# Linear attention and two dense layers on one core: tail projections in row tiles, and a new order of the attention period

## The chip, the cores and the metric

The kernel runs on one core of a Trainium2 chip. The metric is the device time of one execution in microseconds (us), as the median over several runs. TensorE multiplies matrices, VectorE reduces and combines, ScalarE copies and applies functions, GpSimd does elementwise work, and SyncE (SP) issues nearly all transfers. "Array" is TensorE's 128x128 array; a product of 64 rows uses half of its rows, an output of 64 or 32 partitions a part of its columns.

## The reference

```python
def phi(x):
    proj = np.einsum('bhsd,df->bhsf', x, w_phi)
    proj = proj - np.max(np.abs(proj), axis=-1, keepdims=True)
    return np.concatenate([np.exp(proj), np.exp(-proj)], axis=-1)
q_p, k_p = (phi(q), phi(k))
kv = np.einsum('bhsf,bhsd->bhfd', k_p, v)
z = np.sum(k_p, axis=2)
num = np.einsum('bhsf,bhfd->bhsd', q_p, kv)
den = np.einsum('bhsf,bhf->bhs', q_p, z)[..., None] + 1e-06
...
h = x @ w_in
g = h * (1.0 / (1.0 + np.exp(-h)))
return (g @ w_out).astype(np.float32)
```

There are 4 batches of 8 heads, 576 positions, 64 numbers per head and 128 features. The attention output becomes 2304 rows of 512; two dense layers of width 2048 follow, the second with h * cos(h). All is fp32.

## The kernel before

The attention is worked in eight groups `n` of four heads each. Of the 576 positions 512 are the main part and 64 the tail. For one group and one of q and k, `phi` (line 366) projects: `u == 0` is the tail of all four heads, `u == 1` and `u == 2` the main part of two heads each. A main call issues eight products (L380) of 64 rows by 128 columns, in pairs: one takes partitions 0 to 63, the other 64 to 127, and they write the two halves of a PSUM tile `p` of two banks (tag "p", two buffers, so four banks). The tail is one product (L372) over all 128 partitions with 256 columns, against `wf`, a weight of which two quarters are zero (the two heads of a partition block stand in it block by block); it writes one bank of the tag "t2" (two buffers). VectorE then takes the maximum of the absolute values (L384) and subtracts it (L386); the PSUM buffer is free when the subtraction is done.

The other pieces of one group are:

- `kx.u` (k_exp, L402): ScalarE's two exponentials of a k part.
- `qx.u` (q_exp): TensorE transposes of a q part into a "t2" tile (L410, four for the main part, two for the tail), and ScalarE's exponentials (L417, L420).
- `kv.p.c.h` (kv_parts): products for the key-value matrix of head pair `p`, feature half `c`, first or second part `h`. The first part begins with two products of the tail (L436) and goes on with eight of the main part (L439), the second has eight more. They have 64 output columns of the array, and after the last ScalarE copies the result (L443).
- `num.a.half` (L458, four products, 64 columns) and `den.half` (L469, eight products, 32 columns), each into a buffer of the tag "kn" (two buffers, shared with kv) and copied out by ScalarE (L279, L285).
- `load.k`, `load.q`, `load.v`: transfers issued on SP. A group's v goes into `va` (L338, one buffer) and `vt` (L341, two buffers), so most of v can be loaded only when the kv products of the group before are done.
- `inv`, `app`: the reciprocal of `den`, sent through memory to all partitions, and the multiplication with it (GpSimd, L308 and L311), after whose second call for a batch `xd` is stored (L313).
- `piece`: one step of preparing the dense layers' weights (a fetch of raw weights, L139 and L141; an operation or two on ScalarE, VectorE or GpSimd; a store, L199).
- `x.i`: one step of the first dense layer's inputs, in the last two periods.

The order in which the pieces are issued, the same for all engines, is written out by hand in two tables. START is run once and holds the first group's beginning. PERIOD is run for n = -1 to 7; `+` after a name means the next group, `++` the one after. Steps that START already did are skipped. Every engine works its own instructions in that order, and semaphores order them between engines. After the eighth period `moe` begins with products L757.

Of the kernel before, what the change touches and what calls it, by code (L numbers as in the profile page):

```python
# [7 lines left out]
F32 = mybir.dt.float32  # L8
# [7 lines left out]
P = 128  # L16
NQ = 8
B, H, S, D = 4, 8, 576, 64
F = 128
# [14 lines left out]
PB, T2, KN, QB = 2, 2, 2, 2  # L34
# [13 lines left out]
def parse(text):  # L48

    out = []  # L50
    for w in text.split():
        name, *args = w.rstrip("+-").split(".")
        out.append((w.count("+") - w.count("-"), name, *(int(x) if x.isdigit() else x for x in args)))
    return out
# [8 lines left out]
""")  # L63

PERIOD = parse("""
kv.1.1.1 phi.k.2+ num.0.1 num.0.0 num.1.1 load.v+ kx.1+ x.3+ phi.q.1+ den.0 piece x.5+ den.1 num.1.0 phi.q.0+ qx.1+
piece inv kx.2+ kx.3+ phi.q.2+ x.4+ phi.k.1++ kv.0.0.0+ kx.4+ kv.0.0.1+ qx.0+ kv.0.1.0+ piece x.0+ kv.0.1.1+ x.2+
load.q++ qx.2+ x.7++ app.G qx.3+ kv.1.0.0+ x.1++ load.k+++ kv.1.0.1+ x.6+ qx.4+ phi.k.0++ x.8++ kx.0++ kv.1.1.0+ piece
""")


# [244 lines left out]
def attention(tc, q, k, v, w_phi, norm, pieces, then):  # L316
    nc = tc.nc
    W = D + 1
    with ExitStack() as ctx:
# [3 lines left out]
        pp = ctx.enter_context(tc.tile_pool(name="at_ps", bufs=1, space=PSUM))  # L323
# [19 lines left out]
        wf = sp.tile([P, 2 * F], F32, name="wf")  # L343
# [23 lines left out]
        def phi(n, name, u):  # L367

            src = raw[n, name]
            if u == 0:  # L370
                pt = pp.tile([P, 4, P], F32, name="t2", tag="t2", bufs=T2)[:, 0:2]
                nc.tensor.matmul(pt.rearrange("p a f -> p (a f)"), src[:, 0:P], wf, start=True, stop=True)  # L372
                pv, g = pt, 2
            else:
                ps = pp.tile([P, 2, 4, F], F32, name="p", tag="p", bufs=PB)
                c = P + (u - 1) * SM
                for i in range(4):
                    for half in range(2):
                        rows = slice(D * half, D * half + D)
                        nc.tensor.matmul(ps[:, half, i], src[rows, c + i * P:c + (i + 1) * P], wf[rows, half * F:(half + 1) * F],  # L380
                                         start=True, stop=True)
                pv, g = ps.rearrange("p a b f -> p (a b) f"), 8
            m = sp.tile([P, g], F32, name=f"m{g}", bufs=3)
            nc.vector.tensor_reduce(m, pv, axis=AX.X, op=ALU.max, apply_absolute_value=True)  # L384
            t = sp.tile([P, g, F], F32, name="pmt" if u == 0 else "pm", bufs=2 if u == 0 else 3)
            nc.vector.tensor_tensor(t, pv, m.unsqueeze(2).to_broadcast([P, g, F]), op=ALU.subtract)  # L386
            pm[n, name, u] = t
# [87 lines left out]
        def step(n, name, *arg):  # L475
# [14 lines left out]
            elif name == "phi":  # L490
                phi(n, *arg)
            elif name == "kx":
                k_exp(n, *arg)
            elif name == "qx":
                q_exp(n, *arg)
            elif name == "kv":
                p, c, h = arg
                if (n, p) not in kvq:
                    kvq[n, p] = kv_parts(n, p)
                for f in kvq[n, p][9 * c + 5 * h:9 * c + 5 + 4 * h]:  # L500
                    f()
            elif name == "num":
                num(n, *arg)
            elif name == "den":
                den(n, *arg)
            elif name == "warm":
                t = pp.tile([P, 512], F32, name="num", tag="kn", bufs=KN)
                for _ in range(arg[0]):
                    nc.tensor.transpose(t[:, 0:P], ident, ident)
            elif name == "inv":  # L510
                norm.invert(n)
            elif name == "app":
                norm.apply(n, engines[arg[0]])
# [636 lines left out]
```

## Time and profile before

| | us |
|---|---|
| median of 3 runs (941.54 to 944.22) | 941.57 |
| the profiled execution, its own time | 941.5 |
| its span, first to last instruction | 939.4 |
| TensorE busy | 929.7 |
| VectorE busy | 639.5 |
| ScalarE busy | 522.3 |
| GpSimd busy | 173.2 |

The attention lasts to about 165.6 us of the span, the dense layers take the rest. Positions in the text are us from the start of the span. "The chain" is the chain of waits that ended last, followed back through the program: a piece of it on TensorE lasts from the end of the piece before it to its own end, so its lengths add up. The granted TensorE clock of the whole run is 1.00.

### The profile page before, as it was taken

The numbers are of one execution on the slowest core, as the hardware profiler recorded it, in microseconds if no ns is written. First come the engines' busy times: TensorE is split into PE (matmuls) and PEld (weight loads), VectorE is DVE, ScalarE is ACT, GpSimd is POOL, SyncE is SP. The second block draws the span as 40 slices with busy tenths as digits, with TensorE's granted clock in tenths as the row PEclk, the third lists the DMA queues.
The fourth block names the chain that finished last, engine by engine and source line by source line (L and its number), as shares of the span: only waits on it lengthen the run. The fifth ranks groups of instructions, "written<-read, shape, count | busy, mean of one in ns | idle before, by whom it ended". The sixth has DMA issues, their size and how long they took to land.

```text
span 939.4 us, 18064 instructions
## 1 busy us (share of the span) xinstructions
PE 929.7 (99%) x7271; PEld 813.9 (87%) x7271; DVE 639.5 (68%) x961; ACT 522.3 (56%) x944; POOL 173.2 (18%) x142
## 2 busy tenths in 40 slices
PE   8999999999999999999999999999999999999998
PEld 7777776889899998999888988988988989889996
DVE  5777656886647568874456688588786796556556
ACT  4666767866444455565544557463644556544452
POOL 0112342017261711532512500000000000000000
PEclk9999999999999999999999999999999999999999
DMA  5654665566555569798878774633466356342402
GB/s 169 214 141 104 171 193 169 163 231 243 176 225 180 218 227 321 270 370 305 306 277 317 258 291 180 209 128 135 170 226 232 117 198 224 112 157 90 136 1 89
DMA packets 95490, 186.52 MB, mean 199 GB/s; under 512 B 27952, under 2 KB 56752, under 8 KB 94640
## 3 DMA queue, kind: packets, MB, share of 16 engines
q1 hardware_dynamic: 95264, 185.25, 57.6%
q8 instruction: 57, 0.93, 0.4%
q14 instruction: 25, 0.20, 0.1%
q10 hardware_dynamic: 144, 0.13, 0.0%
HBM read 128.06 MB, written 57.22 MB: 197 GB/s over the span
## 4 chain that ended last, share of the span: by engine, by line
PE 97%; DMA 1%; DVE 1%; ACT 1%; issue 0%; SPq 0%
PE h L757 38%; PE y L826 7%; PE y L828 7%; PE y L827 7%; PE y L833 7%; PE y L832 7%; PE y L831 7%; PE p L380 4%; PE num L458 3%; PE kv L439 3%; PE t L410 2%; PE num L469 2%; PE kv L436 1%; PE t L372 1%; DMA vt<-in_v 0%; DMA wf<-in_w_phi 0%
## 5 line engine op out<-in xcount | busy, mean ns | idle before, releaser
L757 PEld LDWEIGHTS h<-xo,w 128*128 128x128 f32 x2688 | 330.0, 188 | 11.6 <-DVE u L970 2.2
L757 PE MATMUL h<-xo,w 128*128 128x256 f32 x2688 | 334.5, 281 | 2.0 <-DVE u L970 1.1
L826 PE MATMUL y<-gh,w 128*128 128x512 f32 (+1 forms) x320 | 119.3, 373 | 0.0
L828 PE MATMUL y<-gh,w 128*128 128x512 f32 (+1 forms) x320 | 118.9, 372 | 0.0
L827 PE MATMUL y<-gl,w 128*128 128x512 f32 (+1 forms) x320 | 118.7, 371 | 0.0
L833 PE MATMUL y<-w,gl 128*128 128x512 f32 x288 | 113.9, 395 | 0.0
L832 PE MATMUL y<-w,gh 128*128 128x512 f32 x288 | 113.6, 394 | 0.0
L831 PE MATMUL y<-w,gh 128*128 128x512 f32 x288 | 113.4, 394 | 0.0
L777 DVE TENSOR_TENSOR gl<-ta,gh 128x512 fp32r<-128x512 f32 x72 | 62.2, 863 | 61.1 <-ACT gh L775 61.0
L782 ACT ACTIVATE tb<-tb 128x512 f32<-128x512 f32 x72 | 45.6, 634 | 92.6 <-DVE tb L781 92.6
L861 DVE TENSOR_TENSOR xa<-y,xa 128x512 f32<-128x512 f32 (+1 forms) x114 | 70.5, 655 | 23.7 <-PE y L828 17.5
L781 DVE SCALAR_TENSOR_TENSOR tb<-tb,ta 128x512 f32<-128x512 f32 x72 | 49.3, 685 | 48.9 <-ACT tb L791 48.9
L191 POOL TENSOR_TENSOR w<-stage,w 128x512 fp32r<-128x512 f32 x48 | 66.7, 1400 | 42.3 <-ACT w L187 36.3
L828 PEld LDWEIGHTS y<-gh,w 128*128 128x128 f32 x320 | 60.1, 188 | 11.2
L826 PEld LDWEIGHTS y<-gh,w 128*128 128x128 f32 x320 | 60.2, 188 | 9.5 <-ACT xa L859 0.2
L827 PEld LDWEIGHTS y<-gl,w 128*128 128x128 f32 x320 | 60.2, 188 | 9.4
L833 PEld LDWEIGHTS y<-w,gl 128*128 128x128 f32 x288 | 54.0, 188 | 12.8
L832 PEld LDWEIGHTS y<-w,gh 128*128 128x128 f32 x288 | 54.0, 188 | 10.8
L831 PEld LDWEIGHTS y<-w,gh 128*128 128x128 f32 x288 | 54.1, 188 | 10.5
L191 POOL TENSOR_TENSOR w<-wt,w 128x512 fp32r<-128x512 f32 x24 | 39.7, 1656 | 125.6 <-ACT w L187 125.6
L775 ACT CAST gh<-ta 128x512 fp32r<-128x512 f32 x72 | 44.7, 621 | 27.8 <-PE y L828 26.0
L235 POOL TENSOR_TENSOR stage<-stage 128x512 f32<-128x512 f32 x28 | 40.7, 1454 | 82.2 <-DVE stage L179 81.8
(103 smaller groups left out, 1384.9 us busy)
## 6 DMA issues: line engine op xcount, KB each, us to landing
w<-d SPq DMA_DIRECT2D x48, 512.0 KB, 5.4
raw_in<-in_moe_w_in SPq DMA_DIRECT2D x32, 512.0 KB, 5.8
raw_out<-in_moe_w_out SPq DMA_DIRECT2D x32, 512.0 KB, 4.5
d<-w SPq DMA_DIRECT2D x32, 512.0 KB, 5.9
rb<-rd SPq DMA_DIRECT2D x16, 288.0 KB, 4.5
va<-in_v SPq DMA_DIRECT2D x32, 128.0 KB, 6.0
yd<-xa SPq DMA_DIRECT2D x4, 1024.0 KB, 3.9
xo<-yd SPq DMA_DIRECT2D x32, 128.0 KB, 4.8
```

The source lines that it names most:

```text
L191: e.tensor_sub(lo, t, hi.bitcast(F32))
L757: nc.tensor.matmul(dst[:, ab], w[:, a, ab, c * P:(c + 1) * P], o[:, b, idx, c], start=start and n == 1, stop=n == 12, skip_group_check=True)
L777: return [silu, lambda: nc.vector.tensor_sub(lo, a, hi.bitcast(F32))]
L781: nc.vector.scalar_tensor_tensor(b, b, MAGIC, a, op0=ALU.subtract, op1=ALU.subtract)
L782: nc.scalar.activation(b, b, AF.Sin, scale=-2.0 * math.pi)
L826: nc.tensor.matmul(o, w[:, 0, at], hi[:, f, x], stop=False, **st)
L827: nc.tensor.matmul(o, w[:, 0, at], lo[:, f, x], start=False, stop=False)
L828: nc.tensor.matmul(o, w[:, 1, at], hi[:, f, x], start=False, stop=en)
L831: nc.tensor.matmul(o, hi[:, f, at], w[:, 0], stop=False, **st)
L832: nc.tensor.matmul(o, hi[:, f, at], w[:, 1], start=False, stop=False)
L833: nc.tensor.matmul(o, lo[:, f, at], w[:, 0], start=False, stop=en)
L861: nc.vector.tensor_tensor(v, o, v, op=ALU.add)
```

## The change

The tail projection becomes two products of 64 rows by 128 columns, one for each half of the partitions, without the zero quarters of `wf`. They write the first block of each half of a "p" tile, so the tail no longer uses "t2". The table PERIOD is written in another order; START is the same.

```diff
 PERIOD = parse("""
-kv.1.1.1 phi.k.2+ num.0.1 num.0.0 num.1.1 load.v+ kx.1+ x.3+ phi.q.1+ den.0 piece x.5+ den.1 num.1.0 phi.q.0+ qx.1+
...
+phi.k.2+ kv.1.1.1 piece num.0.1 num.1.1 phi.q.0+ x.3+ load.v+ kx.1+ phi.q.1+ den.0 den.1 kx.4+ num.0.0 x.5+ num.1.0
...
             if u == 0:
-                pt = pp.tile([P, 4, P], F32, name="t2", tag="t2", bufs=T2)[:, 0:2]
-                nc.tensor.matmul(pt.rearrange("p a f -> p (a f)"), src[:, 0:P], wf, start=True, stop=True)
+                pt = pp.tile([P, 2, 4, F], F32, name="p", tag="p", bufs=PB)[:, :, 0]
+                for a in range(2):
+                    rows = slice(D * a, D * a + D)
+                    nc.tensor.matmul(pt[:, a], src[rows, 0:P], wf[rows, a * F:(a + 1) * F], start=True, stop=True)
                 pv, g = pt, 2
```

TensorE, around the border of two periods, before: the transposes of `qx.4`, the tail and then the main part of k (`phi.k.0`, `phi.k.2`) with the last kv product group between them, the three `num`, and `phi.q.1` (kr and qr are the loaded k and q, kv the key-value products, t the transposes).

```order
L410 MATMUL t_973<-ident,pm 128x128 x4
L372 MATMUL t_980<-wf,kr 128x256
L436 MATMUL kv<-vt_206,kpt 64x130 x2
L439 MATMUL kv<-va,kp 64x65 x16
L380 MATMUL p<-wf,kr 128x128 x8
L458 MATMUL num<-qh_836,kv_931 64x288 x8
L458 MATMUL num<-qh_837,kv_1010 64x288 x4
L380 MATMUL p<-wf,qr 128x128 x8
```

The same place in the changed kernel (its lines are two higher from L374 on):

```order
L412 MATMUL t_992<-ident,pm 128x128 x4
L374 MATMUL p<-wf,kr 128x128 x2
L382 MATMUL p<-wf,kr 128x128 x8
L441 MATMUL kv<-va,kp 64x65 x8
L460 MATMUL num<-qh_846,kv_939 64x288 x4
L460 MATMUL num<-qh_847,kv_1030 64x288 x4
L374 MATMUL p<-wf,qr 128x128 x2
L382 MATMUL p<-wf,qr 128x128 x8
```

Tail and main part of k now stand side by side, as do tail and main part of q; the last kv part runs straight into two of the `num`, and the third `num` has moved behind `den`.

TensorE, in the middle of a period, before: `phi.q.2` and `phi.k.1`, then kv of the first head pair in two parts with the tail's transposes between them, and four transposes twice.

```order
L380 MATMUL p<-wf,qr 128x128 x8
L380 MATMUL p<-wf,kr 128x128 x8
L436 MATMUL kv<-vt_206,kpt 64x130 x2
L439 MATMUL kv<-va,kp 64x65 x16
L410 MATMUL t_903<-ident,pmt 128x128 x2
L436 MATMUL kv<-vt_206,kpt 64x130 x2
L439 MATMUL kv<-va,kp 64x65 x16
L410 MATMUL t_935<-ident,pm 128x128 x4
L410 MATMUL t_945<-ident,pm 128x128 x4
```

And in the changed kernel:

```order
L412 MATMUL t_864<-ident,pmt 128x128 x2
L382 MATMUL p<-wf,qr 128x128 x8
L382 MATMUL p<-wf,kr 128x128 x8
L438 MATMUL kv<-vt_206,kpt 64x130 x2
L441 MATMUL kv<-va,kp 64x65 x16
L438 MATMUL kv<-vt_206,kpt 64x130 x2
L441 MATMUL kv<-va,kp 64x65 x16
L412 MATMUL t_944<-ident,pm 128x128 x4
L412 MATMUL t_951<-ident,pm 128x128 x4
```

The tail's transposes have moved ahead, next to those of `qx.1`, and the two kv parts stand together.

SyncE's queue in the sixth period, where the next group's v is loaded behind the store of `xb`, before and then after:

```order
L331 DMA qr<-in_q 128x1152
L313 DMA xd_66<-xb 128x2048
L199 DMA d00S_77<-w_165 128x1024
L338 DMA va<-in_v 128x4x64 x4
L341 DMA vt_207<-in_v 64x64 x4
```

```order
L331 DMA qr<-in_q 128x1152
L199 DMA d00S_77<-w_165 128x1024
L313 DMA xd_66<-xb 128x2048
L338 DMA va<-in_v 128x4x64 x4
L341 DMA vt_207<-in_v 64x64 x4
```

The store of a prepared weight has moved ahead of the store of `xb`.

## Rows read from the trace of the kernel before

**Rows 1.** The page's first part: busy time of each engine.
```profile
PE 929.7 (99%) x7271; PEld 813.9 (87%) x7271; DVE 639.5 (68%) x961; ACT 522.3 (56%) x944; POOL 173.2 (18%) x142
```
**Rows 2.** The chain over one period: start us, us, what.
```profile
43.89 1.09 PE p L380 x16
44.98 3.06 PE num L458 x24
...
49.13 2.08 PE num L469 x32
51.21 1.12 PE num L458 x8
52.33 0.63 PE t L372 x2
...
53.40 1.98 PE p L380 x32
55.38 0.37 PE kv L436 x4
55.75 0.94 PE kv L439 x32
56.69 0.37 PE t L410 x2
...
58.37 1.02 PE t L410 x8
...
60.69 0.59 PE t L410 x4
61.28 0.53 PE t L372 x2
...
63.11 1.09 PE p L380 x16
```
**Rows 3.** The chain at the end of START.
```profile
22.91 0.47 PE kv L439 x16
23.38 0.59 PE t L410 x4
23.96 0.62 PE kv L439 x16
```
**Rows 4.** TensorE's instructions in order of time, in START.
```profile
18.45 0.39 PE L436 MATMUL kv<-vt,kpt 128*64 128x130 f32 x4
18.67 0.64 PE L439 MATMUL kv<-va,kp 128*64 128x65 f32 x16
```
**Rows 5.** VectorE's instructions in order of time, after k's tail and main projection.
```profile
42.62 0.42 DVE L384 TENSOR_REDUCE m<-t 128x2 f32<-128x256 f32 x1 [1.28 <-PE t L372]
...
45.03 1.23 DVE L384 TENSOR_REDUCE m<-p 128x8 f32<-128x1024 f32 x1 [0.93 <-PE p L380]
46.29 1.23 DVE L386 TENSOR_TENSOR pm<-p,m 128x1024 f32<-128x1024 f32 x1
```
**Rows 6.** ScalarE's instructions in order of time, in the same place.
```profile
43.62 0.72 ACT L402 ACTIVATE kpt<-pmt 128x256 f32<-128x256 f32 x2 [0.35 <-DVE pmt L386]
44.25 0.36 ACT L443 COPY kv<-kv 128x260 f32<-128x260 f32 x1
```
**Rows 7.** The chain at the last period's projection, and at the dense layers' start.
```profile
140.02 1.09 PE p L380 x16
...
165.60 3.03 PE h L757 x24
```
**Rows 8.** TensorE's instructions in order of time, before the last group's kv.
```profile
152.18 0.44 PE L436 MATMUL kv<-vt,kpt 128*64 128x130 f32 x4 [1.56 <-DMA vt<-in_v]
```
**Rows 9.** TensorE's waits up to 165 us: for what, us in total, times, longest.
```profile
PE kv L436 <- DMA vt<-in_v: 1.6, 1, 1.6
```
**Rows 10.** SyncE's issues in order of time, in the sixth period.
```profile
142.17 0.32 SPq L313 DMA_DIRECT2D xd<-xb  x1
```
**Rows 11.** The chain at the start of the span.
```profile
4.43 1.22 PE t L372 x2
```

More of the change, by code (lines that the diff above doesn't have):

```diff
@@ L65 @@
 PERIOD = parse("""
-kv.1.1.1 phi.k.2+ num.0.1 num.0.0 num.1.1 load.v+ kx.1+ x.3+ phi.q.1+ den.0 piece x.5+ den.1 num.1.0 phi.q.0+ qx.1+
-piece inv kx.2+ kx.3+ phi.q.2+ x.4+ phi.k.1++ kv.0.0.0+ kx.4+ kv.0.0.1+ qx.0+ kv.0.1.0+ piece x.0+ kv.0.1.1+ x.2+
-load.q++ qx.2+ x.7++ app.G qx.3+ kv.1.0.0+ x.1++ load.k+++ kv.1.0.1+ x.6+ qx.4+ phi.k.0++ x.8++ kx.0++ kv.1.1.0+ piece
+phi.k.2+ kv.1.1.1 piece num.0.1 num.1.1 phi.q.0+ x.3+ load.v+ kx.1+ phi.q.1+ den.0 den.1 kx.4+ num.0.0 x.5+ num.1.0
+piece qx.1+ inv kx.2+ kx.3+ x.4+ qx.0+ phi.q.2+ phi.k.1++ kv.0.0.0+ kv.0.0.1+ kv.0.1.0+ piece load.q++ x.0+ kv.0.1.1+
+piece qx.2+ qx.3+ x.2+ x.7++ app.G kv.1.0.0+ kv.1.0.1+ x.1++ load.k+++ x.6+ kv.1.1.0+ qx.4+ phi.k.0++ x.8++ kx.0++
 """)
```

## The prediction

> **What bounds the kernel now.** I read the page's busy times first: TensorE is busy 929.7 of 939.4 us and no other engine over 68% [rows 1], so what counts is how TensorE's time is filled. Then I read the chain of waits through the attention, the only stage that the change touches. Through a whole period it never leaves TensorE: from 43.89 to 63.11 us one piece follows another, 19.22 us in all [rows 2]. Up to 165 us TensorE waits for loaded v once, 1.56 us before the last group's kv [rows 8, 9], and its other waits there lie in START. A saving therefore has to come out of the lengths of those pieces, and a new wait costs in full.
>
> The pieces hold something that is no work. One main projection takes 1.09 us, two in a row 1.98 [rows 2]: the second costs 0.89, so 0.20 of the first is something else. Three `num` take 3.06 and one 1.12: 0.97 each, and 0.15 once. Eight transposes take 1.02 and two 0.37: 0.108 each, and 0.15 once. A half kv part after transposes takes 0.62, after its own kind 0.47 [rows 3]: 0.15 again. The two tail products of kv take 0.37 after another kind [rows 2], but 0.22 after kv (18.45 to 18.67) [rows 4]: 0.15. So a change of tile size (64 rows, 64 columns, 32 columns, whole array) costs 0.15 us, and 0.20 into 64 rows, while pieces of one size join at no cost. By the order, a period has 14 such changes before and 11 after.
>
> **The tails.** L372 takes 0.63 us behind `num`: 0.20 for its change and 0.43 of work. Behind transposes, where no change is due, it takes 0.53 [rows 2], 0.10 more than its work; I read that as a wait for its "t2" buffer. The pair of 64-row products isn't in the trace. Eight main products of its shape are four pairs in 0.89 us, so a pair takes 0.22 if it runs together, and 0.43 if it doesn't. I take 0.22, as the main products are the same instruction, and keep 0.43 for the range.
>
> **One period, summed.** In the new order, each size change in front of its piece: tail of k 0.42, main 0.89, second half of the last kv part 0.62, two `num` 1.94, tail of q 0.42, main 0.89, two `den` 2.08, two `num` 2.09, six transposes 0.80, two main projections 1.98, kv 1.30 and 1.15, eight transposes 1.02, kv 1.30, half a part 0.69, four transposes 0.59. That is 18.18 us, 1.04 less than 19.22: 0.42 from two tails, 0.1 from the "t2" wait, 0.5 from three size changes.
>
> **All periods.** Before, from the last kv half of START (23.96) to the dense layers (165.60) [rows 3, 7] are 141.64 us, of which 1.56 is the wait for v, so 140.08 of work. After: the first period lacks the tail of k, which START has done (17.96); five whole ones (90.90); the seventh lacks the main projection of a next group (17.29); the eighth has only the last kv half, `num` and `den` (0.62 + 1.94 + 2.08 + 2.09 = 6.73). Sum 132.88: **7.2 us less**.
>
> **The wait for v.** The last v is late since SP holds its loads behind the store of `xb`, issued at 142.17 [rows 10], and v lands just before 152.18, some 10 us later [rows 8]. That store hangs on the chain den, reciprocal, broadcast and GpSimd, none of it shortened. From `den` to the kv that needs v TensorE now takes about 22.2 us, where it had 22.5, so the wait would grow to 1.9. But a weight store of 512 KB now stands ahead of `xb`'s, not between it and v, and can be gone before. I take 0.8, with 0 and 1.9 as ends: **0.8 us less**.
>
> **START.** Its first tail takes 1.22 us [rows 11], a pair 0.22; what follows waits partly for VectorE and ScalarE. The gain lies between 0 and 1.4 (the 1.0, and 0.4 of a wait between transposes for "t2", which the tail leaves). I take **0.5 less**.
>
> **New waits.** The tails move into the two buffers of "p", six calls a period where four were. The main q projection now needs the buffer of the main k projection two calls before. VectorE starts to read that at its end (44.98 to 45.03) and is done 2.54 us later, at 47.52 [rows 5]. In the new order 0.62 + 1.94 + 0.42 = 2.98 us lie between, and a product starts up to 0.25 earlier than my ends show, so 0.2 is left. The second `num` now follows the kv group after one `num`. Its copy stands on ScalarE behind the exponentials of the k tail (43.62) and ends at 44.61 [rows 6], 2.0 us after VectorE has begun on that tail at 42.62 [rows 5]; 0.89 + 0.62 + 0.97 = 2.48 lie between, so again some 0.2. Both hold on paper with nothing to spare. I charge 0.1 per period, **0.7 us more**.
>
> Here the Trainium skill speaks against the change: "TensorEngine Tiling (Array Packing)", Gotcha 1: PSUM Pressure, says that row tiling raises the demand on PSUM, since different row tiles write different banks. The trace agrees so far that a two-bank tile is held 2.5 us after its projection. By that rule the sum would be the one of the second rival.
>
> **What else is moved.** In the first period four weight fetches of 512 KB go onto SP ahead of v instead of behind it; SP reaches them while TensorE is still in START, so they can run early. Later a weight fetch or store stands before a load of k; k is needed a period later. GpSimd gets one addition of weights ahead of `app` in some periods, at cost nothing since it is busy 18% [rows 1]; if that cover fails, `xb` and the last v come 1.3 us later. The dense layers' instructions keep their order, so they only shift.
>
> **Sum.** 7.2 + 0.8 + 0.5 - 0.7 = 7.8 us less than the profiled execution's own 941.5, which stands 0.07 under the median: 933.7 us.
>
> **The rivals.**
> - *The new order saves nothing.* If the 0.15 and 0.20 belong to each kind of piece and not to the size, only the tails save: 14 in the periods by 0.21, and START's 0.5, 3.4 in all: 938.1. For it: the price into 64 rows is not that of the others. Against it: the half kv part and the kv tail products show both lengths for the same piece.
> - *"p" becomes the bound.* The tail of k now ends just ahead of the main part, and VectorE reads it first, in two operations of 0.42 us [rows 5]. If the main part's read-out comes later by those 0.8 us in each period, less the 0.2 spare, the q projection waits 0.6 us instead of 0.1; seven times 0.5 is 3.5: 937.2. For it: the read-out of the tail does stand in front. Against it: the main products run 0.89 us, in which VectorE can finish the tail.
> - *v comes late in every period: slower.* The new order leaves 10.2 us between the end of kv and the next group's kv; most of v can be loaded only in there. In the last period the landing came 12.1 us after that end (140.02 to about 152.1) [rows 7, 8]. At that lag each of seven loads costs 1.9 us, 13.4 in all: 947.1. It decides against the change from a mean lag of about 11.4 us on, where seven times 1.2 us eat the gain. Against it: of all loads before only one was waited for [rows 9], and that one stood behind `xb`.
> - *The change doesn't do what it says:* the pair runs one after the other. That costs 0.21 for each of 14 tails, 2.9 us: 936.6.
>
> **How the numbers follow.** The forecast gets 0.64, the order that saves nothing 0.10, "p" as the bound 0.12, late v 0.06, the serial pair 0.04; 0.04 is left for losses at the start of the dense layers. The low end is the forecast with no wait for v (0.8), START at its best (0.9) and no new waits (0.7): 931.3. The high end takes in the first two rivals and the serial pair: 938.5. Faster by over 0.3% (which is about what a measurement can tell from no change) means under 938.7: 0.86, nearly all of the cases but late v. Within 0.3%: 0.08. Slower: 0.06, late v.
>
> **What would show it.** In the chain a period should be near 18.2 us, the main projections behind a tail 0.89 instead of 1.09, kv behind kv 1.15 instead of 1.30, two transposes of the tail no longer a piece of their own. TensorE should have no wait for VectorE at the q projection, and the one for v should be shorter. The dense layers should start near 157.8 us. A period near 18.7 with VectorE as releaser means the second rival, one of 19 us with whole pieces at their old lengths the first, and waits for v in many periods the third. I would be wrong altogether if the periods shortened and the dense layers took the time back.

## The result and the profile after

The changed kernel takes 932.58 us (median of 4 runs, 931.74 to 932.8), the kernel before beside it 941.56 (4 runs, 940.28 to 944.22): a ratio of 0.9899, 95% interval [0.9877, 0.9922], 9.0 us less. Two more measurements of the same kernel gave 932.61 and 931.92 (ratios 0.9897 [0.9879, 0.9915] and 0.9889 [0.9872, 0.9905]). The forecast was 933.7, with a range of 931.3 to 938.5.

The profiled execution's own time is 931.74, its span 929.6. The busy times on the page, against [rows 1]:

```profile
PE 919.8 (99%) x7303; PEld 809.2 (87%) x7303; DVE 641.5 (69%) x961; ACT 521.8 (56%) x944; POOL 170.1 (18%) x142
```

TensorE has lost 9.9 us of busy time, the span 9.8. Its idle time is the same in sum (9.7 and 9.8 us): new waits stand where the one for v was, and the saving lies in TensorE's pieces, which became shorter. Not all of that is the edit: TensorE ran the beginning of START at a higher rate in this execution (see below). The chain of waits over one period (start us, us, what) answers to [rows 2]; a product of the program counts twice in these rows, so x16 is the eight products of a main part, while a transpose counts once:

```profile
40.60 0.89 PE p L382 x16
41.49 0.61 PE kv L441 x16
42.11 1.94 PE num L460 x16
44.05 0.42 PE p L374 x4
44.47 0.89 PE p L382 x16
45.37 2.08 PE num L471 x32
47.44 2.09 PE num L460 x16
49.53 0.81 PE t L412 x6
...
53.63 0.22 PE kv L438 x4
53.85 0.93 PE kv L441 x32
...
58.39 0.42 PE p L374 x4
58.81 0.89 PE p L382 x16
```

The period runs from 40.60 to 58.81, 18.21 us, where it took 19.22. Both main projections behind a tail take 0.89 instead of 1.09, kv behind kv 0.22 + 0.93 = 1.15, six transposes in one piece 0.81, and the two products of a tail 0.42, of which 0.20 is their size change. No engine but TensorE stands in this stretch. The chain at the end of the last period and the start of the dense layers, against 165.60 in [rows 7]:

```profile
150.30 0.29 ACT kv L445
...
150.63 1.19 PE num L460 x8
...
155.99 3.04 PE h L759 x24
```

The dense layers start 9.61 us earlier. From there to the end are 773.6 us, where there were 773.8, with the same busy times of every engine to within 3 us: they only shifted. Part of the 9.61 lies in START: its last four transposes end at 22.19 instead of 23.96 [rows 3], 1.77 less. From there to the dense layers are 133.80 us instead of 141.64, 7.84 less. TensorE's waits up to 170 us (for what, us in total, times, longest), against [rows 9], which was the wait for v:

```profile
PE p L374 <- DVE pm L388: 0.9, 1, 0.9
...
PE p L382 <- DMA qr<-in_q: 0.7, 1, 0.7
...
PE num L460 <- ACT kv L445: 0.4, 1, 0.4
```

The first two lie in START. The third is new: in the last period the second `num` waits for the copy at 150.30. The wait for v is gone: against [rows 8], no wait stands behind the first kv row of the last group.

```profile
142.43 0.44 PE L438 MATMUL kv<-vt,kpt 128*64 128x130 f32 x4
```

### The profile page after: what moved, and what is told of

Same layout as the page of the kernel before. It is cut to its first block, busy times and chain, and to the rows that moved or that the text cites. A ratio compares the mean times of both kernels' runs of the same rounds, so it can differ in the third digit from the quotient of the medians.

```text
span 929.6 us, 18114 instructions
## 1 busy us (share of the span) xinstructions
PE 919.8 (99%) x7303; PEld 809.2 (87%) x7303; DVE 641.5 (69%) x961; ACT 521.8 (56%) x944; POOL 170.1 (18%) x142
## 4 chain that ended last, share of the span: by engine, by line
PE 97%; DVE 1%; ACT 1%; DMA 0%; issue 0%
PE h L759 39%; PE y L828 7%; PE y L830 7%; PE y L829 7%; PE y L835 7%; PE y L834 7%; PE y L833 7%; PE num L460 3%; PE kv L441 3%; PE p L382 3%; PE t L412 2%; PE num L471 2%; PE kv L438 1%; PE p L374 1%; DMA wf<-in_w_phi 0%; DVE m L386 0%
## 5 line engine op out<-in xcount | busy, mean ns | idle before, releaser
L386 DVE TENSOR_REDUCE m<-p 128x8 f32<-128x1024 f32 (+1 forms) x48 | 45.8, 954 | 26.8 <-PE p L374 18.1
L191 POOL TENSOR_TENSOR w<-wt,w 128x512 fp32r<-128x512 f32 x24 | 35.8, 1493 | 127.9 <-ACT w L187 118.6
```

What stands on the lines that cost most here:

```text
L191: e.tensor_sub(lo, t, hi.bitcast(F32))
```

## The experiments

Nine measurements were made beside the kernel before, in three groups (the first four, three and two of the table); the median of the kernel before was 941.31, 941.86 and 942.23 us.

| | median us | runs | ratio to before | 95% |
|---|---|---|---|---|
| tails only | 939.25 | 10 | 0.9976 | 0.9964 to 0.9989 |
| order only | 936.98 | 5 | 0.9948 | 0.993 to 0.9965 |
| read twice | 940.63 | 10 | 0.9984 | 0.9973 to 0.9995 |
| store behind | 934.53 | 4 | 0.9917 | 0.9896 to 0.9939 |
| four `num` together | 937.29 | 6 | 0.9948 | 0.9929 to 0.9967 |
| changed, again | 932.61 | 6 | 0.9897 | 0.9879 to 0.9915 |
| store behind, again | 934.29 | 4 | 0.9915 | 0.9893 to 0.9937 |
| tail of q later in START | 932.79 | 4 | 0.9899 | 0.9884 to 0.9914 |
| changed, third time | 931.92 | 4 | 0.9889 | 0.9872 to 0.9905 |

### The tails alone, the order alone

The first keeps the row-tile tails and puts the old table PERIOD back; the second keeps the new table and puts L371 and L372 of the kernel before back:

```diff
-                pt = pp.tile([P, 2, 4, F], F32, name="p", tag="p", bufs=PB)[:, :, 0]
-                for a in range(2):
...
+                pt = pp.tile([P, 4, P], F32, name="t2", tag="t2", bufs=T2)[:, 0:2]
+                nc.tensor.matmul(pt.rearrange("p a f -> p (a f)"), src[:, 0:P], wf, start=True, stop=True)
```

> The old order of the period, with the tail projections as two products of 64 rows. Theory (a change of tile size costs 0.15 to 0.20 us, and joined pieces of one size cost none): in the old order the pair stands between pieces of other sizes, so it brings a change of its own. Tail and transposes of q go from 1.07 to 0.42 + 0.59 = 1.01, tail of k from 0.53 to 0.42: 0.17 us a period, a period of 19.05 us, 1.2 us over seven periods, and with up to 1.8 us at the start and the wait for v still 1.6 us about 938.5 to 940.5 us. Rival (the tails alone save and the order nothing): 0.52 us a period, a period of 18.70 us, 936 to 937 us.

> The new order of the period, with each tail as one product of 128 rows and 256 columns in its old buffer. Theory (size changes): the tail of q stands between num and the main projection of q with two changes, 0.63 + 1.09 instead of 1.31; the tail of k joins the transposes before it, 0.43 to 0.53 + 1.09 instead of 1.31; a period of 18.83 to 18.93 us where the whole change has 18.21, and 938 to 939.5 us in all with the old start. Rival (the order saves nothing of itself): a period of 19.2 us and 940 to 941.5 us.

The chain with the tails alone, from one border of two periods to the next:

```profile
60.41 0.37 PE kv L438 x4
...
61.72 1.09 PE p L382 x16
...
79.05 0.42 PE p L374 x4
79.47 0.37 PE kv L438 x4
```

The period is 19.06 us, 0.16 less than before. The tail takes its 0.42, but kv stands between it and the main part, which pays its own 0.20. The chain with the order alone:

```profile
60.20 1.09 PE p L380 x16
...
63.85 0.63 PE t L372 x2
64.48 1.09 PE p L380 x16
...
78.60 0.43 PE t L372 x2
79.03 1.09 PE p L380 x16
```

Here it is 18.83, 0.39 less. The tail now stands beside the main part, but is a product of 128 rows, so the main part still pays 0.20, and the tail of q 0.20 of its own. Together the two halves save 1.01 a period, though singly only 0.16 + 0.39 = 0.55: the tails have to be 64 rows deep *and* to stand beside the main part before a border goes away. The time of the order alone was lower than expected (936.98 against 938 to 939.5). Its profile shows no wait for v, and its START, which has the old tails, ends at 22.54 instead of 23.96.

The tails alone keep the old order of the stores, and yet no wait there is put down to v. Before the last group's kv, at 149.69, TensorE waits as follows, against [rows 9]:

```profile
PE kv L438 <- ACT kp L404: 0.6, 1, 0.6
```

Whatever ended it (a late v may hide in it), it is about 1.0 less than the 1.56 before, without the new order.

### How much room the new order leaves in "p"

VectorE reads the main part of k (`u == 2`) twice for its maximum, so the buffer of "p" comes free 1.24 us later in each period:

```diff
+            if name == "k" and u == 2 and n > 0:
+                nc.vector.tensor_reduce(m, pv, axis=AX.X, op=ALU.max, apply_absolute_value=True)
```

> The changed kernel, in which VectorE takes the maximum of the main k projection (second part) twice in every period, 1.23 us more in front of the release of its buffer; the outputs stay the same. Theory (the main q projection waits for that buffer with 0.2 to 0.3 us to spare): TensorE waits 0.9 to 1.0 us for VectorE in each of seven periods, 6.5 to 7 us more than the changed kernel, about 939 us. Rival (VectorE has more room than that): below 1 us more, periods of 18.2 us.

It took 8.1 us more than the changed kernel. The chain now passes through VectorE:

```profile
63.26 1.24 DVE m L388
64.52 1.23 DVE pm L390
...
65.79 1.16 PE p L382 x16
...
85.14 1.16 PE p L382 x16
```

The period is 19.35 us, 1.14 more for the 1.26 of added reading (63.26 to 64.52): the changed kernel has about 0.1 us to spare here. A waited-for main part takes 1.16 where one that follows its tail adds 0.89, so the seven waits that the list of waits shows, 0.8 us each, are 0.3 each less than what they cost.

### Where the wait for v went

`app.G` stands ahead of the period's fourth `piece`, so that SP has the store of `xb` ahead of the weight store again, as before the change. It was run twice:

```diff
-piece qx.2+ qx.3+ x.2+ x.7++ app.G kv.1.0.0+ ...
+app.G piece qx.2+ qx.3+ x.2+ x.7++ kv.1.0.0+ ...
```

> The changed kernel with the multiplication app ahead of the last weight step of the period, so that the store of xb stands on SyncE ahead of the weight store again, as before the change. Theory (the weight store between xb and v made v late): TensorE waits 1.0 to 1.6 us for v before the last group, 933.6 to 934.2 us. Rival (the chain to the store of xb has itself become shorter): no wait for v, and the changed kernel's time within 0.3 us, 932.6.

> The changed kernel with app.G ahead of the period's fourth piece, so that the store of xb stands ahead of the weight store in SP's queue again, as before the change, once more. Theory (the order of the two stores moves the last v by about 1 us): a wait for v of 0.5 to 1.5 us before the last group's kv, and 1 to 2 us more than the changed kernel of the same call. Rival (the wait in the earlier run of this edit came from a slower way of the denominators through memory): no wait for v in this profile, and under 0.8 us more than the changed kernel.

They took 1.95 us more than the changed kernel (by its first measurement) and 1.68 more (in the same group). TensorE in the last period, first run:

```profile
145.13 0.44 PE L438 MATMUL kv<-vt,kpt 128*64 128x130 f32 x4 [1.32 <-DMA vt<-in_v]
...
148.84 0.63 PE L412 MATMUL t<-ident,pm 128*128 128x128 f32 x4 [0.59 <-DVE pm L388]
```

And second run:

```profile
143.44 0.44 PE L438 MATMUL kv<-vt,kpt 128*64 128x130 f32 x4 [0.23 <-DMA vt<-in_v]
...
147.22 0.63 PE L412 MATMUL t<-ident,pm 128*128 128x128 f32 x4 [0.67 <-DVE pm L388]
```

In the second run the wait for v is smaller than expected (0.23 against 0.5 to 1.5); what I had not expected is the second wait, in both. SP issues the load of `den` behind the v loads. It lands late, and VectorE, which stands at the reciprocal (L295) waiting for it, reads the main part of q behind that, for which the transposes wait. VectorE's rows of the first run:

```profile
145.81 0.18 DVE L295 TENSOR_SCALAR r<-den 128x18 f32<-128x18 f32 x1 [4.94 <-DMA den<-dn]
...
146.20 1.16 DVE L386 TENSOR_REDUCE m<-p 128x8 f32<-128x1024 f32 x1
```

So a late `xb` store costs twice. What moves v is seen on SP. The changed kernel's issues (start, us, line, what):

```profile
120.79 0.60 SPq L288 DMA_DIRECT2D den<-dn  x1
...
123.33 0.34 SPq L298 DMA_DIRECT2D rd<-r  x1
124.77 1.12 SPq L301 DMA_DIRECT2D rb<-rd  x2
...
127.08 0.85 SPq L199 DMA_DIRECT2D d00S<-w  x1
132.38 0.32 SPq L313 DMA_DIRECT2D xd<-xb  x1
```

The same issues in the kernel before, whose `xd` stands in [rows 10]:

```profile
128.61 0.60 SPq L288 DMA_DIRECT2D den<-dn  x1
...
131.20 0.34 SPq L298 DMA_DIRECT2D rd<-r  x1
134.51 1.12 SPq L301 DMA_DIRECT2D rb<-rd  x2
```

Two things add up. From the issue of `xd` to v at TensorE: 10.0 us before (142.17 to 152.18), 10.4 and 10.2 with the store behind. Where the weight store stands ahead, the only profile in which v is waited for is that of the next experiment, and there it is 9.0 (137.86 to 146.83); in the order alone TensorE takes v 9.2 us behind `xd` (137.73 to 146.89) and does not wait. From the load of `den` to `xd`: 13.6 us in the profile of before, 11.6 in that of the changed kernel; it is 11.5 to 11.6 with the second read and the later tail of q, 11.7 to 11.9 with the tails alone, the four `num` together, the second store behind and the changed kernel again and a third time, 12.6 and 13.1 in the first store behind and the order alone. It differs between executions of one edit (12.65 and 11.70 with the store behind). Of the 2.0 between 13.6 and 11.6, 1.9 lie in one step, from the store of the reciprocals (`rd`) to the load of their broadcast (`rb`): it takes 3.3 and 3.0 us in the two profiles with the old tails (before, and the order alone) and 1.4 in the nine with the new ones. That the tails shorten it isn't shown, since in other periods the same step takes from 1.4 to 3.9 us with the new tails too; nor is it shown to be chance. TensorE needs v 21.6 us after the load of `den` (120.79 to 142.43).

### One size change fewer

All four `num` stand together, and the main part of q ahead of its tail; this was to beat both kernels:

```diff
-phi.k.2+ kv.1.1.1 piece num.0.1 num.1.1 phi.q.0+ x.3+ load.v+ kx.1+ phi.q.1+ den.0 den.1 kx.4+ num.0.0 x.5+ num.1.0
+phi.k.2+ kv.1.1.1 piece num.0.1 num.1.1 num.0.0 num.1.0 phi.q.1+ x.3+ load.v+ kx.1+ phi.q.0+ den.0 den.1 kx.4+ x.5+
```

> The changed kernel with all four num calls of a period together, and with them phi.q.1 ahead of phi.q.0. TensorE then has one size change fewer in a period, 10 instead of 11: num behind den goes, and of q the main half stands behind num and the tail behind it. Theory (a change of tile size costs 0.15 us, and nothing else in the order counts): period 18.06 instead of 18.21, over seven periods some 1.0 us less than the changed kernel, 931.5 by the medians. Rival (what counts is the room between one use of a buffer and the next, the size changes are worth less): the main half of q now ends just ahead of its own transposes by den alone, 2.1 us, and VectorE's two read-outs take 2.5 us behind it; the transposes of qx.1 would then wait in every period by up to 0.15 to 0.5 us with VectorE as releaser, and the time is that of the changed kernel or up to 2 us more. The period's length in the chain, and whether TensorE's waits name VectorE at the transposes, tell the two apart.

```profile
60.09 0.89 PE p L382 x16
...
61.60 3.88 PE num L460 x32
65.48 1.12 PE p L382 x16
...
69.47 0.44 DVE pmt L388
...
69.95 0.44 PE t L412 x2
...
78.86 0.89 PE p L382 x16
```

Four `num` take 3.88 instead of 1.94 + 2.09, the 0.15 that a size change costs. But the period is 18.77: between the projections of q and their transposes only `den` is left, 2.08 us, and VectorE needs until 69.91 for its four operations. From 65.48 to the end of the transposes are 4.91 us, where the same pieces took 0.42 + 0.89 + 2.08 + 0.81 = 4.20. The rival held, and its loss was under-sized: 0.56 a period, 3.9 in seven periods, and 4.7 us in all against the changed kernel of the same group. In the changed order the two late `num` cover VectorE.

### The changed kernel again, and its START

> The changed kernel as it is, once more, beside the other runs of this call. Theory (the periods are set by the order and are the same in every execution; the START of an execution is not): period 18.21 us, no wait for v or one under 0.5 us, and in START either the first tail projection in 0.52 us and the end of START's kv near 22.2, or 0.80 us and an end near 23.5; the time 931.5 to 933 us accordingly. Rival (the wait for v was only avoided by chance in the one profile): a wait for v of 1 us or more, and 933.5 to 934.5 us in most executions.

> The changed kernel as it is, a third time, beside the run with the START edit. Theory: 931.7 to 933.8 us, median near 932.6, period 18.21 us; START's end and single waits for loads (0.5 us) are what differs from one execution to the next. Rival (the two profiles so far are not typical): a median over 933.5 or under 931.5.

Both medians are within 0.7 us of the first, and neither profile shows a wait for v. The profiled execution of the second measurement is the slowest of its six, 933.81. In it TensorE starts slowly, and once, before the tail of q at 64.24, it waits 0.48 us for a load of q; why that came late isn't shown. TensorE in order of time, at its start:

```profile
4.94 0.80 PE L374 MATMUL p<-wf,kr 64*128 64x128 f32 x4 [0.76 <-DMA wf<-in_w_phi]
5.53 1.92 PE L382 MATMUL p<-wf,kr 64*128 64x128 f32 x16
```

The first profile of the changed kernel at its start:

```profile
4.56 0.49 PE L374 MATMUL p<-wf,kr 64*128 64x128 f32 x4 [0.38 <-DMA wf<-in_w_phi]
4.89 1.06 PE L382 MATMUL p<-wf,kr 64*128 64x128 f32 x16
```

And the kernel before:

```profile
5.58 2.08 PE L380 MATMUL p<-wf,kr 64*128 64x128 f32 x16
```

The same eight products (sixteen instructions) take 1.06 us in one execution and 1.92 in another of the same kernel. The eight of q behind them take 1.92 too in the second profile, and 1.09 in the third, where the first eight took 1.90. With these rates START's last transposes end at 22.19 in the first profile, 23.69 in the second and 23.16 in the third, against 23.96 before.

The last edit takes START's wait of 0.87 us for a buffer of "p" away, by moving one name:

```diff
-... phi.k.2 phi.q.0 load.k+ kv.0.0.0 kv.0.0.1 qx.1 ...
+... phi.k.2 load.k+ kv.0.0.0 kv.0.0.1 phi.q.0 qx.1 ...
```

> The changed kernel with one name of START moved: the tail of q (phi.q.0) behind the two parts of kv.0.0. In the changed kernel's profile it waits 0.87 us for a buffer of p, which VectorE frees at 10.9. Theory (that wait lies on the path of START, since TensorE has kv to do meanwhile): the wait goes, a size change into 64 rows (0.20) comes, and ScalarE's exponentials behind give back only a part; START's end, and with it the whole time, comes 0.4 to 0.7 us earlier than in the changed kernel of the same call at the same rate of TensorE's start. Rival (START is bound by VectorE's read-outs and ScalarE's exponentials, not by that wait): the wait reappears before a later kv with ScalarE as releaser, and the time is that of the changed kernel within 0.2 us.

```profile
14.69 0.44 PE L412 MATMUL t<-ident,pmt 128*128 128x128 f32 x2 [1.17 <-DVE pmt L388]
```

It took 0.87 us more than the changed kernel beside it (932.79, runs from 932.3 to 933.38, against 931.69 to 932.61), so there is no gain. That the edit itself costs 0.87 isn't shown: START ends at 22.71 here, and at 22.80 and 22.90 in the two profiles with the unedited START whose first main products were about as slow (1.48 us here, 1.51 with the tails alone, 1.61 in the second store behind). The wait reappears, as the rival says, but its releaser is VectorE, not ScalarE: it reads the tail of q last, and its transposes wait. None of the versions tried beats the changed kernel.

## Why the prediction was right

**The periods** (7.2 less) came as summed: 18.21 us against 18.18, nearly every piece with its forecast length. That the price belongs to the size change and not to the kind of piece is shown by the two halves: they save 0.16 and 0.39 alone and 1.01 together, where prices of kinds would add up. This ends the first rival (19 us). The fourth, pairs that run one after the other, would have shown a tail of 0.63; it took 0.42.

**"p" as the bound** didn't come, but by little: of the "some 0.2" that I read off the rows, 0.1 is there. The prediction named the rule of the Trainium skill, "TensorEngine Tiling (Array Packing)", Gotcha 1: PSUM Pressure, that row tiling raises the demand on PSUM. The run with the second read agrees, with the bound 0.1 us away. The 937.2 that the prediction gave for it didn't come.

**New waits** (0.7 more, "0.1 per period") came to 0.9, but in another place. Behind START the pieces were summed to 132.88, and 133.80 were measured. Seven periods account for 0.2 of the difference, about 0.03 each, which is no more than the rounding of the sum. Another 0.11 stands in the seventh, where eight transposes take 1.13. The other 0.58 came once, in the eighth period: the second `num` waits 0.37 for its copy, and then takes 1.19 where 0.97 was summed, much the same price of starting afresh (0.22) as in the run with the second read (0.27). I had named that wait, but behind the exponentials of the k tail; it stands behind the exponentials of the last q part and a cast for the dense layers (L575), which only the last periods have.

**The wait for v** (0.8 less) is a term that was mis-sized: all of the 1.56 went. The step that failed is that I took the way from `den` to `xd` as fixed ("none of it shortened") from the one profile, where it was 13.6, the longest in all eleven profiles. With 11.6 and the 9.0 of the experiment, an estimate from those rows, v lands 20.6 us after the load of `den`, a microsecond before TensorE needs it. With before's 13.6 it would be 22.6, a wait of about 1, near the 0.8 forecast. So the low end, no wait for v, was the right one. The part of it that I had reasoned out is the weight store that is gone before: 9.0 to 9.2 us from `xd` to v against 10.0 to 10.4. The shorter way I had not foreseen, and it may be luck: with the tails alone, where the way took 11.7, TensorE waited only 0.6 in that place, so some 1.0 of the 1.56 went there without the new order.

**Late v in every period** didn't come: no profile with the new order shows a wait for v ahead of the last one.

**START** (0.5 less) gave 1.77 in the two profiles, but most of it is TensorE's rate at the start, not the edit. Of the slow starts, the second profile of the changed kernel ends 0.27 us before the kernel before, and that of the first store behind, with the same START, 0.46 (23.50). Of the fast ones, the order alone, with the old tails in the same START, ends at 22.54, the changed kernel at 22.19: 0.35. So the edit is worth about 0.3 to 0.5, and the rest of 1.77 came by chance. The 1.22 us that I had read for the first tail held the slow rate as well: the same product takes 0.70 in the order alone, and the pair, which I put at 0.22, takes 0.52 in the fast start and 0.80 in a slow one.

**The sum.** Between the two profiled executions lie 9.8 us, 2.0 more than the 7.8 forecast: 0.8 from v, 1.3 from START, 0.2 from the dense layers, less 0.2 of new waits. Between the medians lie 9.0, 1.2 more than forecast: 0.8 from v less 0.2, and 0.6 that no run assigns, START's rate and the spread of the executions (the kernel before alone ran from 940.28 to 944.22).

**Left open:** why TensorE starts slowly in some executions, and why the way of `den` through memory to `xd` differs by 2 us, by chance or by the tails.

## What to carry to other kernels

Sum a TensorE-bound stretch piece by piece from the chain, and look for the same piece at two lengths: the difference is what the border costs, and it goes only if both sides get one tile size and stand together. Before you remove one more border, ask what the piece between covers: here the two `num` behind `den` cover VectorE's read-out, and moving them to save 0.15 us cost 0.7. A transfer's lateness that is read from one profile may not come again (the way to `xd` took from 11.5 to 13.6 us here): keep its other end in the sum.

## What the runs showed of the hardware that I had not expected

TensorE's first products run at about half the rate in some executions of one kernel (the eight of k's main part in 1.92 us) and at the full rate in others (1.06), after the same twelve transposes and a wait of 0.3 to 0.8 us; that is near the ratio of its two levels, 1.2 and 2.4 GHz. The granted clock of these stretches reads 1.00 in every profile, so the rows don't show the cause. The Trainium skill, "TensorE: Matmul & The Clock Gate", Part 1: The HAM clock gate (the "warmup" mystery), says that the number of slow first products differs between runs of one kernel; the rows agree in that: in the profiles of the changed kernel neither, both or only the first of the two main parts at the start are slow, and START's end lies up to 1.5 us apart.
